# Transposes ahead of the conditioning matmuls, filler matmuls, and two tiny early loads in an adaLN attention and SwiGLU kernel

## The chip, the cores and the metric

The kernel runs on one core of a Trainium2 chip. The metric is device time in microseconds (us) of one execution. The *span* is the time from the first to the last instruction; it is about 2.0 us shorter than the device time. Each timed execution also lists its span and its mean granted TensorE clock (1.000 is full speed).

## The reference, cut to what matters

```
mod = (silu(c) @ w_mod) -> six vectors sa, ca, ga, sb, cb, gb of 1024
h   = layernorm(x) * (1 + ca) + sa                # x: 2048 x 1024
x   = x + ga * linear_attention(h, wqkv, wo)
h   = layernorm(x) * (1 + cb) + sb
x   = x + gb * (silu(h @ w_gate) * (h @ w_up) @ w_down)
```

The study is about the first 27 us: the first four 128-row tiles of x are normalised and transposed, the vectors ca and sa are computed from w_mod as they arrive, and the first matmuls of q begin.

## The kernel before: the parts that matter

All loads go out on the SyncE queue, in this order. None of those shown waits on a computation.

```python
P.dma("c", CS8[0:NDT, :], cv8)
for st in range(4):
    P.dma("x0_%d" % st, XRES[:, st, :], xv[:, st, :])      # 256 KB each, 2 KB rows
...
for p in range(4):
    ca_load(p)        # "wca": 256 columns of the scale part of w_mod, 512 KB in 512-byte rows
    sa_load(p)        # "wsa": the same of the shift part
    if p < 3:
        wq_load(p)    # 512 KB of the q weights, 2 KB rows
```

I number these loads from 0: wca0, wsa0, wq0, ..., wca3, wsa3. The first computations, in TensorE's order:

```python
warm(11, bank=3)                 # filler matmuls, to have the clock granted
mod_sc(WCA, 8, range(2))         # 16 matmuls of one column; wait for wca0
warm(3, bank=3)
... layer norm of tiles 0 and 1 (VectorE), of 2 and 3 (also ScalarE) ...
tile_transposes(0)
...
mod_sc(WSA, 0, range(2))         # wait for wsa0
tile_transposes(1)
...
h0_first(0, 0, "dve")            # scale and shift: the first input of q
...                              # then q matmuls; mod_pair(1), (2), (3) between them
```

`mod_pair(p)` computes the vectors from wca *p* and wsa *p*. TensorE reaches `mod_pair(3)` after the first four of seven column groups of its third pass over q.

## Time and profile before

| | before |
|---|---|
| time, median of 3 | 840.45 us (840.42 to 840.97) |
| span of the profiled execution | 838.5 us |
| TensorE busy | 825.3 us (98%) |
| TensorE's waits for wca in the head | 2.7 us |
| TensorE's waits for wsa in the head | 0.2 us |
| granted clock 9 to 15 us | 0.50 |

This is TensorE's timeline of the kernel before. The columns are start, duration, engine, line, operation, output and inputs, form and count; in brackets stand the idle time before it and what ended it.

```profile
2.76 3.87 PE L178 MATMUL ps<-e_92,ident 128*128 128x512 bf16 x11 [0.37 <-DVE e_92 L178]
9.38 0.59 PE L178 MATMUL ps<-siluc,wca 128*128 128x1 bf16 x16 [2.75 <-DMA wca<-in_w_mod_dram]
...
11.06 1.06 PE L178 MATMUL ps<-ident,xres 128*128 128x128 bf16 x8
11.91 0.61 PE L178 MATMUL ps<-siluc,wsa 128*128 128x1 bf16 x16
12.39 1.01 PE L178 MATMUL ps<-ident,xres 128*128 128x128 bf16 x8
13.59 2.29 PE L178 MATMUL ps<-ht,wqk 128*128 128x256 bf16 x10 [0.19 <-DVE ht L178]
...
26.52 0.55 PE L178 MATMUL ps<-siluc,wsa 128*128 128x1 bf16 x16 [0.18 <-DMA wsa<-in_w_mod_dram]
```

Two things strike the eye: the gap of 2.75 us at 9.38, and the short wait for wsa3 at 26.52.

The next view is a table of stretches of the kernel before: stretch, length, busy time of TensorE, weight loads, VectorE, ScalarE and GpSimd (instructions started), granted clock, DMA share, GB/s.

```profile
4.00:5.00 1.00, 1.00 (x4) 0.43 (x3) 0.95 (x2) 0.00 (x0) 0.00 (x0) 1.00 1.08 227
5.00:6.00 1.00, 1.00 (x5) 0.37 (x4) 1.00 (x3) 0.00 (x0) 0.00 (x0) 1.00 0.85 265
9.00:10.00 1.00, 0.62 (x17) 0.56 (x18) 0.12 (x2) 0.97 (x3) 0.55 (x1) 0.50 1.12 307
14.00:15.00 1.00, 1.00 (x6) 0.72 (x5) 1.00 (x3) 0.46 (x1) 0.00 (x0) 0.50 1.14 318
```

The clock is at half from 9 us on, and the DMA engines are full. (The table counts time before the first clock record as 1.00. The fillers there start 0.43 us apart until 5.5 us and 0.21 us apart afterwards, so the clock was first granted at about 5.5 us.) At 4 to 6 us the stream is slower than later.

The chain of waits, in order of time, says what 26.52 depended on (start, duration, what):

```profile
17.38 0.47 SPq L178
17.85 0.04 issue
17.89 8.58 DMA wsa<-in_w_mod_dram
26.48 0.04 issue
26.52 2.84 PE ps L178 x26
```

Back of 26.52 there is only SyncE's queue and the load.

### The profile page before, as it was taken

The page shows a single profiled execution, that of the slowest core. Times are in us where ns is not written, and L with a number is a line of the kernel's source. Part 1 is how long each engine was busy: PE and PEld are TensorE (multiplying, and loading weights), DVE is VectorE, ACT ScalarE, POOL GpSimd, SP SyncE. Part 2 cuts the span into 40 slices and gives each one's busy share as a digit, 9 for nine tenths or more (in the row PEclk, how much of TensorE's full clock was granted, in tenths as well). Part 3 has the DMA queues.
Part 4 walks back from the last instruction along what each step waited for, and adds up shares of the span by engine and source line. Part 5 has one row for each costly group of instructions (what it writes and reads, how often), then busy time and mean ns, then how long its engine had stood idle before and what let it go on. Part 6 is the DMA issues. An engine that isn't in the chain of part 4 may idle for free.

```text
span 838.5 us, 10210 instructions
## 1 busy us (share of the span) xinstructions
PE 825.3 (98%) x4154; PEld 384.1 (46%) x4233; DVE 298.3 (36%) x641; ACT 203.8 (24%) x355; POOL 41.0 (5%) x52
## 2 busy tenths in 40 slices
PE   7999999999999999999999999999999999999998
PEld 4444444454444444444444444444444444444444
DVE  5777966556974212111221111022121102111111
ACT  4667763213333111100111111021111101111111
POOL 1000000000050000030000003000000300000000
PEclk8999999999999999999999999999999999999999
DMA  9993323747195895540355562045556104553000
GB/s 276 265 323 48 68 89 126 172 136 265 37 248 184 266 296 155 153 80 26 108 153 153 151 157 58 24 114 151 151 150 181 46 13 113 151 152 99 1 25 26
DMA packets 178125, 112.99 MB, mean 135 GB/s; under 512 B 32664, under 2 KB 161824, under 8 KB 178080
## 3 DMA queue, kind: packets, MB, share of 16 engines
q1 hardware_dynamic: 178080, 112.35, 48.1%
q8 instruction: 33, 0.54, 0.3%
q14 instruction: 12, 0.10, 0.0%
HBM read 100.67 MB, written 4.33 MB: 125 GB/s over the span
## 4 chain that ended last, share of the span: by engine, by line
PE 95%; SPq 2%; DMA 1%; DVE 1%; issue 1%; ACT 0%; DVEq 0%
PE ps L178 95%; SPq L178 2%; DMA wsa<-in_w_mod_dram 1%; DVE acc L178 0%; DVE xres L178 0%; DVE mhl L178 0%; ACT mw L178 0%; DVE ve_72 L178 0%; DVE ut L178 0%; DVE mean_70 L178 0%; DVE msq_71 L178 0%; DVE sumx L178 0%; DVEq L249 0%
## 5 line engine op out<-in xcount | busy, mean ns | idle before, releaser
L178 DVE TENSOR_TENSOR at<-sg,ps 128x512 bf16<-128x512 bf16 x112 | 77.0, 688 | 296.1 <-PE ps L178 285.1
L178 ACT ACTIVATE sg<-ps 128x512 bf16<-128x512 f32 x112 | 66.9, 597 | 310.3 <-PE ps L178 298.9
L178 PE MATMUL ps<-wd_a,at 128*128 128x512 bf16 (+2 forms) x519 | 112.8, 372 | 0.5
L178 PE MATMUL ps<-wd_b,at 128*128 128x512 bf16 (+2 forms) x388 | 85.4, 372 | 0.5
L178 PEld LDWEIGHTS ps<-wd_a,at 128*128 128x128 bf16 x528 | 51.1, 98 | 59.8
L178 DVE TENSOR_TENSOR ut<-att,gb_b 128x512 bf16<-128x512 bf16 (+1 forms) x32 | 13.5, 421 | 167.7 <-ACT att L178 167.7
L178 ACT ACTIVATE att<-ps 128x512 bf16<-128x512 f32 (+1 forms) x32 | 17.4, 591 | 182.1 <-PE ps L178 182.1
L178 PE MATMUL ps<-ht,wqk 128*128 128x512 bf16 (+1 forms) x258 | 58.4, 376 | 1.0 <-DVE ht L178 0.5
L178 PEld LDWEIGHTS ps<-wd_b,at 128*128 128x128 bf16 x396 | 38.3, 98 | 44.7
L178 PE MATMUL ps<-wqk,ht 128*128 128x512 bf16 x250 | 56.6, 379 | 0.4
L178 PE MATMUL ps<-mw,pqt 128*128 128x512 bf16 x250 | 55.8, 379 | 0.4
L178 PE MATMUL ps<-h2t,guu_117 128*128 128x512 bf16 x221 | 52.8, 379 | 0.2
L178 PE MATMUL ps<-h2t,guu_115 128*128 128x512 bf16 x219 | 52.6, 379 | 0.3
L178 PE MATMUL ps<-h2t,gug_114 128*128 128x512 bf16 x220 | 52.6, 379 | 0.2
L178 PE MATMUL ps<-h2t,guu_116 128*128 128x512 bf16 x221 | 52.6, 379 | 0.2
L178 PE MATMUL ps<-h2t,gug_111 128*128 128x512 bf16 x220 | 52.5, 379 | 0.2
L178 PE MATMUL ps<-h2t,gug_112 128*128 128x512 bf16 x219 | 52.5, 379 | 0.2
L178 PE MATMUL ps<-h2t,gug_113 128*128 128x512 bf16 x219 | 52.3, 379 | 0.3
L178 PE MATMUL ps<-h2t,guu_118 128*128 128x512 bf16 x217 | 52.1, 379 | 0.3
L178 POOL TENSOR_SCALAR h2t<-h2t,modcol 128x512 bf16<-128x512 bf16 x32 | 28.3, 898 | 394.4 <-DMA h2t<-xn_119 394.4
L178 ACT ACTIVATE e_92<-ps 128x512 bf16<-128x512 f32 x64 | 39.1, 611 | 30.8 <-PE ps L178 27.0
L178 ACT ACTIVATE rl<-ps 128x512 bf16<-128x512 f32 x64 | 38.9, 608 | 0.0
(120 smaller groups left out, 685.5 us busy)
## 6 DMA issues: line engine op xcount, KB each, us to landing
gug_111<-in_B_w_gate_dram SPq DMA_DIRECT2D x14, 512.0 KB, 4.0
guu_115<-in_B_w_up_dram SPq DMA_DIRECT2D x14, 512.0 KB, 5.3
gug_112<-in_B_w_gate_dram SPq DMA_DIRECT2D x14, 512.0 KB, 4.0
guu_116<-in_B_w_up_dram SPq DMA_DIRECT2D x14, 512.0 KB, 5.3
gug_113<-in_B_w_gate_dram SPq DMA_DIRECT2D x14, 512.0 KB, 4.0
guu_117<-in_B_w_up_dram SPq DMA_DIRECT2D x14, 512.0 KB, 5.3
gug_114<-in_B_w_gate_dram SPq DMA_DIRECT2D x14, 512.0 KB, 4.1
guu_118<-in_B_w_up_dram SPq DMA_DIRECT2D x14, 512.0 KB, 5.3
```

Source lines behind the costliest of these rows:

```text
L178: return getattr(e, method)(**kw)
```

## The change

The intent is to use TensorE's idle time ahead of wca0 for both tiles' transposes, to keep its clock with fillers, and to pay the first access to w_mod and wqkv early with two tiny loads ("touches") of 32 bytes of every eighth row. The diff, cut to its core:

```diff
+        P.dma("tm", TOUCH[0:16, 0:8, :], wmv[0:128:8, :, 0:16], queue="act")
+        P.dma("tq", TOUCH[0:16, 8:16, :], wqkvv[0:128:8, :, 0:16], queue="act")
         P.dma("c", CS8[0:NDT, :], cv8)
 ...
-        warm(11, bank=3)
-        mod_sc(WCA, 8, range(2))
-        warm(3, bank=3)
         fa = fin_ca(0)
+        warm(13, bank=3)
 ...
         tile_transposes(0)
+        warm(2, bank=3)
         s1_[2]()
         ln1_rstd1(1)
         s3_[0]()
+        ln1_xn(1)
+        tile_transposes(1)
+        warm(0, bank=3)
+        mod_sc(WCA, 8, range(2))
+        warm(4, bank=3)
 ...
         mod_sc(WSA, 0, range(2))
-        tile_transposes(1)
+        warm(3, bank=3)
 ...   (tile 2 is normalised earlier, one copy moves up; bookkeeping for loads on the ScalarE queue)
```

More of the change, by code (lines that the diff above doesn't have):

```diff
@@ L96 @@
 class _Op:
-    __slots__ = ("idx", "eng", "fn", "deps", "signaled", "count", "semkey", "waits", "ninc", "tag")
+    __slots__ = ("idx", "eng", "fn", "deps", "signaled", "count", "semkey", "waits", "ninc", "tag", "isdma")
     def __init__(self, idx, eng, fn, semkey, ninc, tag):
@@ L109, in __init__ @@
         self.tag = tag
+        self.isdma = semkey.startswith("lane:")
 def _is_ap(v):
@@ L129, in add @@
     def add(self, eng, fn, reads=(), writes=(), lane=None, ninc=1, tag=None):
-        if eng in self.COMPUTE:
-            semkey = eng
-        else:
-            assert lane is not None
-            semkey = "lane:" + lane
+        semkey = eng if lane is None else "lane:" + lane
+        assert eng in self.COMPUTE or lane is not None
         op = _Op(len(self.ops), eng, fn, semkey, ninc, tag)
@@ L165, in add @@
         self.by_eng.setdefault(eng, []).append(op)
-        if eng not in self.COMPUTE:
+        if op.isdma:
             self.dma_ops.append(op)
@@ L211, in resolve @@
         for op in self.ops:
-            if op.eng not in self.COMPUTE and op.fn is not None:
+            if op.isdma and op.fn is not None:
                 op.signaled = True
@@ L216, in resolve @@
             if op.signaled:
-                c = counters.get(op.semkey, 0) + (op.ninc if op.eng in self.COMPUTE else 16 * op.ninc)
+                c = counters.get(op.semkey, 0) + (16 * op.ninc if op.isdma else op.ninc)
                 counters[op.semkey] = c
@@ L236, in resolve @@
                 sn = dict(kn)
-                if op.eng in self.COMPUTE:
+                if not op.isdma:
                     sn[op.semkey] = op.count
@@ L253, in body @@
                     if op.signaled:
-                        if eng in self.COMPUTE:
+                        if not op.isdma:
                             r.then_inc(sems[op.semkey], op.ninc)
@@ L327, in bass_adaLN_cond__linear_attn_block__swiglu_ffn__prompt_kernel @@
         RSTD2 = T("rstd2", SM + 2240, [128, NST], FP32)
+        TOUCH = T("touch", 202 * KB, [128, 16, 16], BF16)
         ZCOL = T("zcol", SM + 2304, [128, NHG], FP32)
@@ L620, in bass_adaLN_cond__linear_attn_block__swiglu_ffn__prompt_kernel @@
         neg_rstd(2)
+        m3[1]()
+        m3[2]()
         fa[0]()
-        ln1_xn(1)
+        ln1_xn(2)
         fa[2]()
-        m3[1]()
+        m3[3]()
         fa[4]()
-        m3[2]()
+        m3[4]()
         mod_sc(WSA, 0, range(2))
-        tile_transposes(1)
-        m3[3]()
-        m3[4]()
+        warm(3, bank=3)
+        neg_rstd(3)
         fa[1]()
-        neg_rstd(3)
+        raw_copy(4, 4, 0, "act")
         fa[3]()
@@ L635, in bass_adaLN_cond__linear_attn_block__swiglu_ffn__prompt_kernel @@
         h0_first(1, 0, "dve")
-        raw_copy(4, 4, 0, "act")
         raw_copy(2, 2, 0, "dve")
-        ln1_xn(2)
         ln1_xn(3)
```

## The prediction

> **What bounds it.** TensorE is busy 825.3 of 838.5 us (busy table); the chain of waits is 95% TensorE. The change touches only the first 27 us, so a few microseconds at most are in play.
>
> In that head, the chain of waits, back from the scaling-vector matmuls at 26.52 us, holds no TensorE work: it is SyncE's queue issuing loads up to 17.89, then the last shift-vector load (wsa, 8.58 us in flight, landing 26.48). The DMA stream binds. The table of stretches agrees: DMA share 1.0 to 1.2 from 7 us on, 290 to 360 GB/s. After 26.5 TensorE never again waits long for data.
>
> TensorE loses time earlier: it idles 2.75 us before 9.38 for the first wca, its granted clock is 0.50 from 9 to 15.3 us, and the ten first 256-wide q matmuls take 2.29 us instead of about 1.1. This loss is already repaid before 26.5: the last wait there, 0.18 us, is for DMA.
>
> **What the change does.**
> - It moves both transposes (1.06 and 1.01 us) ahead of the first wca matmuls, and normalised tiles 1 and 2 earlier on VectorE; it adds 8 filler matmuls (0.43 us cold, 0.22 warm). The 2.75 us gap shrinks to well under 1, so by the Trainium skill, "TensorE: Matmul & The Clock Gate", part 1 (clock granted after about 3.4 us of activity, withdrawn after an idle window), the clock should stay at 1.0 where the trace shows 0.50. The first q matmul should move from 13.59 to about 12.6: wsa0 lands at 11.0, wq0 at 12.5.
> - None of this moves a load: SyncE's loads in the head wait on no compute. TensorE, 1 to 2 us earlier, will wait for wsa1 (16.0), wsa2 (21.5), wsa3 (26.5) instead, 2 to 4 us in sum against 0.2. Worth at the end: 0 us.
> - The touches are 256 descriptors of 32 bytes, 16 per DMA engine. From the packet rates (512 bytes: 16 engines x 1.18 / 566 per us = 33 ns; 2 KB: about 96 ns) I estimate 15 to 35 ns each, 0.25 to 0.55 us per engine, partly in idle time before 2.3 us. The Trainium skill, "DMA: Bandwidth & Descriptors", HWDGE ordering, says the ScalarE queue uses the same 16 engines, so this delays the stream: 0 to 0.4 us. ScalarE's table load and silu slip about 0.9 us, off the path.
> - Possible return: at the first accesses to w_mod (4 to 6 us) the stream runs at 227 to 265 GB/s, against about 300 later: 0.3 to 0.45 us lost. If that is a first-access cost, the touches recover it. More likely it is the issuing of many 512-byte descriptors; I give recovery 35%.
>
> **Sum.** The last wsa landing shifts by about -0.1 us (-0.7 to +0.5). Predicted 840.3 us, 8 in 10 between 839.6 and 841.0. Faster by over 2%: 0.01; within: 0.98; slower: 0.01.
>
> **What would show it.** Granted clock 1.0 in 9 to 15 us (else the fillers failed). First q matmul near 12.6. TensorE waits for wsa of 2 us or more in sum. Last wsa landing within 0.6 us of 26.48, the time moving by the same amount. At 4 to 6 us, about 300 GB/s if touching pays, else 230 to 265.
>
> **What would make it wrong.** The new waits could withdraw the clock near 26 us (+1 to 2 us). The touches could be much slower than estimated and hold up the x loads (+1 us). Or the first-access cost is spread over the whole head, and touching brings 1 us or more.

## The result, and the profile after

The changed kernel took 840.04 us (median of 4, 839.95 to 840.74), against 840.43 (840.24 to 840.97) for the kernel before in the same rounds. The ratio is 0.9996, 95% interval 0.9979 to 1.0013: the same. A ratio is the mean time of one kernel's runs over that of the other's of the same rounds, so not quite the ratio of the medians quoted.

TensorE's timeline of the changed kernel:

```profile
2.75 4.67 PE L176 MATMUL ps<-e_93,ident 128*128 128x512 bf16 x13 [0.36 <-DVE e_93 L176]
7.71 0.62 PE L176 MATMUL ps<-ident,xres 128*128 128x128 bf16 x8 [0.28 <-DVE xres L176]
...
9.24 0.62 PE L176 MATMUL ps<-ident,xres 128*128 128x128 bf16 x8 [0.48 <-DVE xres L176]
9.70 0.54 PE L176 MATMUL ps<-siluc,wca 128*128 128x1 bf16 x16
...
11.28 0.55 PE L176 MATMUL ps<-siluc,wsa 128*128 128x1 bf16 x16 [0.16 <-DMA wsa<-in_w_mod_dram]
...
12.83 1.39 PE L176 MATMUL ps<-ht,wqk 128*128 128x256 bf16 x10 [0.32 <-DVE ht L176]
...
25.99 0.55 PE L176 MATMUL ps<-siluc,wsa 128*128 128x1 bf16 x16 [0.85 <-DMA wsa<-in_w_mod_dram]
```

The gap at 9.38 is gone, the first q matmuls start 0.76 us earlier and take 1.39 in place of 2.29 us, and the wait for wsa3 has grown from 0.18 to 0.85 us. The same stretches as before:

```profile
4.00:5.00 1.00, 1.00 (x4) 0.44 (x3) 0.82 (x2) 0.00 (x0) 0.00 (x0) 1.00 1.02 365
5.00:6.00 1.00, 1.00 (x4) 0.32 (x3) 1.00 (x3) 0.34 (x1) 0.00 (x0) 1.00 1.05 310
9.00:10.00 1.00, 0.76 (x20) 0.76 (x21) 0.79 (x7) 0.66 (x3) 0.42 (x1) 1.00 1.01 316
14.00:15.00 1.00, 1.00 (x18) 0.93 (x16) 0.07 (x1) 0.00 (x0) 0.00 (x0) 1.00 1.04 322
```

Once granted, the clock stays at 1.00. The dip at 4 to 6 us is absent, just as if the touches had paid. The chain of waits of the changed kernel:

```profile
17.53 1.21 SPq L176
18.74 0.04 issue
18.78 7.16 DMA wsa<-in_w_mod_dram
25.94 0.05 issue
25.99 34.04 PE ps L176 x213
```

wsa3 landed 0.54 us earlier (25.94 against 26.48), its matmuls began 0.53 us earlier, and the span fell by 0.5 us, from 838.5 to 838.0. From this pair alone one would credit the touches with 0.5 us. The experiments were made to find out whether that is so.

### The profile page after: what moved, and what is told of

Read it like the earlier page. It is cut to its first block, busy times and chain, and to the rows that moved or that the text cites. A ratio compares the mean times of both kernels' runs of the same rounds, so it can differ in the third digit from the quotient of the medians.

```text
span 838.0 us, 10305 instructions
## 1 busy us (share of the span) xinstructions
PE 830.0 (99%) x4241; PEld 383.5 (46%) x4241; DVE 299.5 (36%) x641; ACT 203.9 (24%) x355; POOL 41.2 (5%) x52
## 4 chain that ended last, share of the span: by engine, by line
PE 96%; SPq 2%; DVE 1%; DMA 1%; issue 0%; ACT 0%; DVEq 0%
PE ps L176 96%; SPq L176 2%; DMA wsa<-in_w_mod_dram 1%; DVE acc L176 0%; DVE xres L176 0%; DVE mhl L176 0%; ACT mw L176 0%; DVE ve_72 L176 0%; DVE ut L176 0%; DVE mean_70 L176 0%; DVE msq_71 L176 0%; DVE sumx L176 0%; DVEq L247 0%
## 5 line engine op out<-in xcount | busy, mean ns | idle before, releaser
L176 ACT ACTIVATE att<-ps 128x512 bf16<-128x512 f32 (+1 forms) x32 | 17.4, 591 | 182.1 <-PE ps L176 182.1
```

Of the source, the lines that this page charges most:

```text
L176: return getattr(e, method)(**kw)
```

## The experiments

Theory: the touches move the load stream, the stream's last wsa sets the end, and the reorder by itself is worth nothing. Rivals: the reorder brings the gain; any early traffic helps; or the stream wanders from execution to execution and the pair above is chance.

### Reading a trace of this kernel with one number

In 13 of the 14 traces, the span less the start of the wsa3 matmuls is 811.97 to 812.07 us, for every kernel (for instance 838.5 - 26.52 before, 838.0 - 25.99 after). All that these kernels differ by has happened by that matmul. I call its start the *wsa3 start*. The fourteenth trace is explained below.

### 1 and 2: the new order without touches, twice

```diff
-        P.dma("tm", TOUCH[0:16, 0:8, :], wmv[0:128:8, :, 0:16], queue="act")
-        P.dma("tq", TOUCH[0:16, 8:16, :], wqkvv[0:128:8, :, 0:16], queue="act")
```

> The new order and the fillers, without the two touches. Theory (the touches alone move the load stream, and the end follows the last wsa landing): 840.4 us as before, first wsa3 matmul near 26.5 us, stream at 4 to 6 us at 225 to 265 GB/s; granted clock 1.0 in 9 to 15 us and first q matmul near 12.8 all the same. Rival (the reorder brings the gain, the stream's change is chance): 840.0 us, wsa3 near 26.0.

The first set gave 841.51 us median (840.32 to 841.95). Three of five executions had a granted clock of 0.998 and spans of 839.4 to 839.9; the other two had 1.000 and 838.2. Neither theory had foreseen that. TensorE's timeline of the profiled one:

```profile
20.80 0.55 PE L176 MATMUL ps<-siluc,wca 128*128 128x1 bf16 x16 [0.51 <-DMA wca<-in_w_mod_dram]
22.34 0.55 PE L176 MATMUL ps<-siluc,wsa 128*128 128x1 bf16 x16 [0.99 <-DMA wsa<-in_w_mod_dram]
22.76 4.87 PE L176 MATMUL ps<-ht,wqk 128*128 128x512 bf16 x14
...
27.86 0.54 PE L176 MATMUL ps<-siluc,wsa 128*128 128x1 bf16 x16
```

and its stretches there:

```profile
19.49:22.91 3.42, 1.92 (x37) 1.17 (x36) 0.00 (x0) 0.00 (x0) 0.00 (x0) 1.00 1.02 308
22.91:26.32 3.41, 3.41 (x9) 1.21 (x8) 1.30 (x7) 0.00 (x0) 0.00 (x0) 0.50 1.08 308
```

TensorE, being early, waited 0.51 us for wca2 and 0.99 us for wsa2. It was busy 1.92 of 3.42 us, and for the next 3.41 us its clock was at half. Fourteen q matmuls took 4.87 us where they take 3.26 at full clock, so TensorE reached wsa3 at 27.86 although it had landed at 26.9. This is the risk that the prediction listed, brought about by the new waits.

Was it this kernel or chance? The same kernel was run again.

> The same kernel as the first run of the new order without touches. If the loss of the clock belongs to this kernel: again about three of five executions at 0.998 and 839.4 to 839.9 us span, median 840.3 to 841.5. If it was chance: spans as the changed kernel, 838.0 to 838.5. In the trace, last x load delivered near 6.2 us and the stream behind the touched kernels by 0.3 us or more, if the touches matter; near 5.8 if that was chance too.

This time it took 840.17 us (839.92 to 840.48), all five clocks at 1.000, spans 837.8 to 838.3. So the loss strikes some executions of the same kernel and not others. With the clock kept, the seven executions without touches have a mean span of 838.11 us; the eight executions of the changed kernel with the clock kept (in the result above and in experiment 5) have 838.23. The touches show no gain in timed executions. The trace did not decide between the two forecasts for the x loads: the stream had moved as many bytes as c and x hold at 6.08 us, between 5.8 and 6.2.

### 3: touches alone, in the old order

The edit keeps the two touch lines and restores the old order of TensorE and VectorE.

> The two touches in the old order. Theory: the stream shows 300 GB/s or more at 4 to 6 us and the last wsa lands near 25.9, but TensorE, with a wait of only 0.18 us there before, is not ready before 26.3: the wait for wsa3 vanishes and the time is 840.2 to 840.3, half of the gain or less. Rival (the touches do nothing): 840.4, wsa3 landing at 26.5, 225 to 265 GB/s at 4 to 6 us. Rival 2 (both parts add independently): 840.0.

It took 840.14 us (839.69 to 841.40), kernel before 840.43; ratio 1.0 (0.9987 to 1.0012). wca0 landed at 8.4 us in place of 9.3, so the early gap was shorter and the clock was just kept. But wsa3 landed at 26.3, only 0.2 us earlier than in the first trace. My expectation that TensorE would not be ready and that the wait would vanish was wrong: with the clock kept it was ready, and waited 0.69 us. One us gained at wca0 had shrunk to 0.2 at wsa3. Four of these five executions had a mean clock of 1.000, against 5 of 32 of the kernel before without touches (counted below): an earlier wca0 may save the clock even in the old order. One set of five is thin evidence, and one of the four has a span of 839.4 all the same.

### 4: touches of tensors that the head does not read

```diff
-        P.dma("tm", TOUCH[0:16, 0:8, :], wmv[0:128:8, :, 0:16], queue="act")
-        P.dma("tq", TOUCH[0:16, 8:16, :], wqkvv[0:128:8, :, 0:16], queue="act")
+        P.dma("tm", TOUCH[0:16, 0:8, :], wgv[0:128:8, :, 0:16], queue="act")
+        P.dma("tq", TOUCH[0:16, 8:16, :], wuv[0:128:8, :, 0:16], queue="act")
```

> The changed kernel, with the same two tiny loads of the same shape on the same queue, but of the gate and up weights, which the head does not read. First-access theory: no return, dip to 225 to 265 GB/s at 4 to 6 us, wsa3 near 26.5, 840.4. Rival (any early traffic on the engines or on a second queue helps): as the changed kernel, 840.0, wsa3 near 26.0.

It took 840.35 us (839.95 to 840.75). Its trace is among the fastest, as the timeline at wsa3 shows:

```profile
25.83 0.55 PE L176 MATMUL ps<-siluc,wsa 128*128 128x1 bf16 x16 [0.94 <-DMA wsa<-in_w_mod_dram]
```

The stream ran at 359 and 309 GB/s at 4 to 6 us, though w_mod had not been touched. The first-access theory expected 225 to 265 GB/s and 26.5, so this trace speaks against it. The median of 840.35 does not: it lies nearer to that theory's 840.4 than to the rival's 840.0. One trace is not enough here, as the next experiment shows; the packets below decide.

### 5: the changed kernel again

No edit.

> The changed kernel once more, as the yardstick of this set. Every theory: 840.0 us, wsa3 near 26.0, 310 to 365 GB/s at 4 to 6 us. If wsa3 is near 26.5 here, the landing time wanders from run to run and no single trace of this set proves anything.

It took 840.49 us (840.13 to 841.78), kernel before 840.43. Four clocks were 1.000; one was 0.998, with a span of 839.8. The profiled execution's timeline at wsa3:

```profile
26.49 0.55 PE L176 MATMUL ps<-siluc,wsa 128*128 128x1 bf16 x16 [0.89 <-DMA wsa<-in_w_mod_dram]
```

That is the wsa3 start of the kernel before, from the changed kernel, with a dip to 203 GB/s at 4 to 5 us. This means that the landing wanders by 0.5 us between executions, and the 0.5 us between the first two traces proves nothing about the touches.

### What the packets say about the dip

The trace records every DMA packet. Adding up the bytes of the SyncE queue in order of completion gives the time by which the engines had moved as many bytes as the loads up to a given one hold ("last x done" and so on). It is a count of bytes: single packets of x end later, up to 7.4 us. The landing itself is later too: a load's semaphore is raised 16 times, for wsa3 in the trace of before from 24.21 to 26.48 us, and the last one counts. These numbers are worked out from those records:

```
trace                    second queue     last x done   wca0 done   wca0 - x   wsa3 done
before                   none             6.27          7.88        1.61       24.58
before again             none             5.82          7.44        1.62       24.05
new order, 1st           none             6.25          7.92        1.67       24.82
new order, 2nd           none             6.08          7.80        1.72       24.37
new order, gaps filled   none             6.32          7.95        1.63       24.68
changed                  touches          5.82          7.45        1.63       24.18
changed again            touches          6.20          7.73        1.53       24.48
touches, old order       touches          5.69          7.31        1.62       24.13
touches elsewhere        other tensors    5.77          7.42        1.65       24.03
```

The first 512 KB of w_mod took 1.53 to 1.72 us after the last x in every trace, touched or not. So w_mod had no first-access cost for a touch to recover, beyond 0.1 us. The packets of 512 bytes, which are those of w_mod, say it more directly: the first starts at 5.65 us in the trace of before, and the first 256 take 27 to 30 ns in the mean in all nine traces, touched or not. So the dip at 4 to 6 us belongs to the x loads. In the trace of before a packet of 2 KB takes 84 ns in the median, but seven that began between 4.0 and 5.1 us took 828 to 1444 ns.

From the last x to wsa3 the stream then took 18.2 to 18.6 us in all nine. The wsa3 landing wanders over 1.1 us in these nine traces, 25.8 to 26.9. Of its parts, the end of x wanders over 0.6 us, the way from there to wsa3 over 0.3, and the time until the last engine's share lands (1.8 to 2.2 us) over 0.4. Slow packets are not the general cause of a late x: in the new order's first trace and with the gaps filled x is as late (6.25, 6.32), and no packet before 7 us took over 0.7 us. What makes it late there is open.

Traces with touches of any tensor have x done somewhat earlier (mean 5.87 against 6.15 us), but the ranges overlap, and experiment 10, also with touches, has 6.08. Whether early traffic on a second queue speeds the x loads is open; the timed spans do not show it.

### 6: the new waits filled

To test the cause of the lost clock, filler matmuls of 0.11 us were put into the new waits of the kernel of experiment 1.

```diff
         def mv_pair(p):
+            gap_fill(3 if p == 2 else 0)
             mod_sc(WCA, 8, range(2 * p, 2 * p + 2))
+            gap_fill({2: 3, 3: 6}.get(p, 0))
             mod_sc(WSA, 0, range(2 * p, 2 * p + 2))
```

> The new order without touches, plus filler matmuls of 0.11 us in the new waits: three ahead of the third wca and three ahead of the third wsa vectors, six ahead of the fourth wsa. Theory (in the run without touches three of five executions lost the clock, because the order's new waits of 0.5 and 1.0 us emptied one activity window; the granted clock of those was 0.998 against 1.000, their spans 839.4 to 839.9): with the waits filled no execution loses the clock, all five show 1.000, spans 838.0 to 838.6, median about 840.3 us. Rival (the clock was lost by chance or for another reason): again some executions at 0.998 with spans above 839.3. Rival 2 (fillers sit on the path): every span some 0.3 to 0.7 us longer than 838.2.

All five clocks were 1.000, as the theory has it, but experiment 2 kept its clock too, without fillers, so this is weak evidence. The time was 840.74 us (840.62 to 841.06), spans 838.5 to 839.0. That is the size that the second rival named, but the trace does not show its reason. This is the timeline of the weight loads at wsa3:

```profile
26.73 0.47 PEld L176 LDWEIGHTS ps<-siluc,wsa 128*128 128x128 bf16 x16 [0.32 <-DMA wsa<-in_w_mod_dram]
```

They waited 0.32 us after those of the last filler, for a wsa3 that landed only at 26.69. In this execution the late landing set the end, and the fillers were not on the path. Why every span of this set is longer stays open.

### 7: the kernel before again

> The kernel before once more, with a trace, for the spread of the load stream without touches. Every theory: span minus the start of the fourth wsa vectors' matmuls 812.0 us. Touches matter: stream slow again at 5 to 6.5 us (205 to 265 GB/s), wsa3 at 26.3 or later. Chance: it may be at 300 GB/s there.

It took 840.66 us (840.39 to 840.71), spans 838.4 to 838.7, in its own set 840.44 for the yardstick. The stream was at about 300 GB/s at 5 to 6.5 us without any touch, which is the answer "chance". Its trace corrects the prediction in another point. wsa3 landed at 26.0 us, but the stretches show another loss of the clock:

```profile
18.26:21.67 3.41, 2.19 (x39) 1.45 (x38) 0.00 (x0) 0.00 (x0) 0.00 (x0) 1.00 1.13 329
21.67:25.09 3.42, 3.20 (x8) 1.18 (x8) 1.30 (x7) 0.00 (x0) 0.00 (x0) 0.50 1.18 317
```

and the timeline shows TensorE's arrival at wsa3:

```profile
26.63 0.54 PE L178 MATMUL ps<-siluc,wsa 128*128 128x1 bf16 x16
```

The clock had been withdrawn at 21.67, and TensorE reached wsa3 at 26.63 with no wait. In this execution of the kernel before, TensorE and not the wsa3 landing set the end, 0.6 us late: its chain goes back over the matmuls at half clock to the landing of wsa2 at 21.06.

### The clock, over all executions

The granted clock changes on a grid of 3.41 us whose position differs from execution to execution. With the grid laid over the 13 traces in which I could place it, the withdrawals in the head all followed a window in which TensorE was busy little:

```
TensorE busy in one window   clock in the next
before           0.34        0.50
experiment 10    0.42        0.50
experiment 1     0.56        0.50
experiment 7     0.64        0.50
experiment 3     0.65        1.00
all others       0.69 up     1.00
```

(The window after the loss in the first trace of before was busy 0.86 and the clock stayed at half for one more.) Busy ends are modelled, so 0.64 and 0.65 do not fix the limit that closely. The closest kept case is this window of experiment 3, in the table of stretches:

```profile
6.87:10.28 3.41, 2.22 (x33) 1.25 (x32) 3.08 (x17) 2.49 (x6) 1.47 (x3) 1.00 1.14 329
```

Counting timed executions by their mean clock: the kernel before was below 1.000 in 27 of 32, the new order (experiments 1, 2, 4, 5 and the changed kernel) in 4 of 24. So the new order, fillers included, does what it was meant for; no run has the one without the other. (The 32 are the yardstick runs of three sets and experiment 7; those of the first round are left out, since their clocks are not all listed. The mean clock does not say where in the span the clock was lost.) But those 27 spans reach only from 838.0 to 839.0. In the first trace the loss came early and was made up by the time of wsa3; in experiment 7 it came later and cost 0.6 us. The 4 have 839.4 to 839.9; in the one that was traced (experiment 1) the clock went at 22.9:

| | executions | median us | mean us | median span | clock lost, spans |
|---|---|---|---|---|---|
| before | 32 | 840.52 | 840.52 | 838.40 | 27, 838.0 to 839.0 |
| new order, all | 24 | 840.34 | 840.50 | 838.20 | 4, 839.4 to 839.9 |

The new order wins about 0.2 us in the median and loses it in the mean. Even the 0.2 us are not clear of the wander: when the 56 spans are dealt out at random to two groups of this size, 8% of the deals differ as much. Nor is every long span a lost clock. Two executions of the kernel before (839.4 and 839.7) and one of experiment 3 (839.4) have a mean clock of 1.000; none of them was traced.

### 8 and 9: the first load 0.45 us earlier

The stream begins with the issue of the first x at 1.25 us, behind the tiny load of c. If the stream sets the end, it should start earlier.

```diff
-        P.dma("c", CS8[0:NDT, :], cv8)
+        P.dma("c", CS8[0:NDT, :], cv8, queue="act")     # ahead of the two touches
```

> The changed kernel with the tiny load of c moved from the SyncE queue to the head of the ScalarE queue, so that the first x load is issued at 0.79 us and not at 1.25. Theory (the stream from the first issue to the last wsa sets the end): all landings 0.4 to 0.45 us earlier, wsa3 near 25.7, span 837.5 to 837.9, median 839.6 us. Rival (the engines' slow first packets set the pace whenever the issue comes): no change, 840.0 to 840.2 us.

> The kernel with the load of c at the head of the ScalarE queue, once more. If its lead of 0.5 us over the kernel before is real: all spans 837.6 to 838.1, median 839.7 to 840.0, ratio to before about 0.9992. If it was the luck of one set: spans spread to 838.5 and the median is 840.2.

The two sets gave 839.93 (839.71 to 840.08) and 839.77 us (839.62 to 839.95), kernel before 840.44 and 840.57; ratios 0.9991 (0.9979 to 1.0004) and 0.9993 (0.9979 to 1.0007). All ten clocks were 1.000 and all ten spans 837.6 to 838.1. Without the touches:

> The same without the two touches. Theory (the touches are worth at most 0.1 to 0.3 us, through the x loads' first packets): within 0.2 us of the kernel with them, 839.8 to 840.1. Rival (the touches carry the gain): 840.2 or more, x loads delivered later by 0.3 us or more.

It took 839.85 us (839.63 to 841.17); four spans of 837.6 to 838.3 with the clock kept, and one of 839.1 without. The touches again carry nothing that I can see. Nor did x come later without them: its bytes were done at 5.50 us, against 5.62 and 5.51 with them. Moving c is the steadiest version found, by about 0.7 us against the pooled median of the kernel before (0.45 us in the median span), though the intervals include 1. The landings did not move as expected: wca0 landed at 8.3 and 8.4 us in the traced executions with touches, but wsa3 at 26.0 and 25.9, not 25.7. In the first trace, x0 was done 0.7 us earlier than in the changed kernel, the last x 0.2.

### 10: wsa3 later on purpose

The changed kernel with two later x loads (512 KB) issued ahead of wca3 and wsa3; nothing is added.

```diff
         for p in range(4):
+            if p == 3:
+                x1_load(0)
+                x1_load(1)
             ca_load(p)
```

> The changed kernel with two of the second x loads (2 x 256 KB) issued ahead of the fourth wca and wsa, nothing added or removed. Theory (the last wsa landing sets the end): 0.5 MB at about 350 GB/s is 1.5 us, wsa3 near 27.5, span near 839.5, median 841.5, and span minus start of its matmuls still 812.0. Rival (TensorE or the other loads pace the head): span within 0.3 us of 838.1.

It took 842.55 us (841.15 to 843.21) where 841.5 was expected, ratio 1.0022 (1.0009 to 1.0034). wsa3 landed at 27.6, as expected. The two executions that kept their clock have spans of 839.3 and 839.4, as expected (839.5). Three lost it (840.7 to 841.2), which I had not expected; the profiled one is of these. Its timeline at wsa3:

```profile
27.65 0.55 PE L176 MATMUL ps<-siluc,wsa 128*128 128x1 bf16 x16 [1.15 <-DMA wsa<-in_w_mod_dram]
```

and the two windows around it, in the table of stretches:

```profile
25.12:28.53 3.41, 1.43 (x35) 1.11 (x36) 0.22 (x3) 0.61 (x2) 0.00 (x0) 1.00 1.08 342
28.53:31.95 3.42, 3.42 (x10) 1.19 (x9) 3.28 (x14) 0.00 (x0) 0.59 (x2) 0.50 1.07 360
```

The waits of 0.87 us for wca3 and 1.15 us for wsa3 emptied a window, and the half clock then fell after wsa3. This is the fourteenth trace, with 841.2 - 27.65 = 813.55 in place of 812.0. That a later wsa3 landing moves the end of the new order by as much, unless the clock is lost, is thereby shown. In 11 of the 14 traces the wsa3 matmuls start within 0.05 us of the landing. In the other three (experiments 1, 7 and 11) TensorE comes later than the load.

### 11: longer rows for the scale part of w_mod

Experiment 8 with wca in two loads of 512 columns (1 KB rows), and ten fillers in place of four ahead of wsa0.

> The same with touches, the scale half of w_mod loaded in two pieces of 512 columns (1 KB rows) in place of four of 256 (512-byte rows), and six more fillers for the longer first wait. Theory (the stream to the last wsa binds, and longer rows run faster: 2 MB at about 330 in place of 290 GB/s is 0.8 us): first q matmul near 14.2 us and yet wsa3 near 25.3, span 837.3 to 837.6, median 839.4. If TensorE's remaining work binds once it starts 1.5 us later: wsa vectors without a wait, span 838.0 to 838.8. Rival (row length makes no difference here): wsa3 at 26.0.

The median was 839.69 us (839.50 to 840.86), the lowest; three spans were 837.4 to 837.6, two 838.6 and 838.8. The traced execution is one of the slow ones. wsa3 landed at 25.6 there, but the timeline has:

```profile
26.57 0.54 PE L176 MATMUL ps<-siluc,wsa 128*128 128x1 bf16 x16
```

TensorE came without a wait, 1 us after the landing. Its wsa0 matmuls had begun at 12.64 though wsa0 landed at 11.8, because the ten fillers ran without a gap from 10.48 until then. But that delay was used up before the end: TensorE waited 0.54 us for wsa2, which landed at 22.61, later than in the changed kernel (21.04), and worked without a pause from there to 26.57. Both theories are partly right: the stream got shorter (17.4 us from the last x to wsa3, against 18.2 to 18.6), and in the traced execution wsa2 and TensorE's work after it became the limit.

## Why the prediction was right

- **The time** (840.3, range 839.6 to 841.0) held: 840.04 measured, and the pooled median of the changed kernel's nine executions is 840.21. The range also holds the kernel before (840.43), so the hit by itself tests little. The reason, that the last wsa landing decides and the reorder cannot move that load, is confirmed by experiment 10 and by both traces of the changed kernel, with waits of 0.85 and 0.89 us for wsa3. The constant 812.0 shows only that the end follows the start of these matmuls, whatever released them.
- **"Worth at the end: 0 us"** was read off one execution. In that one, DMA came last at 26.52; in experiment 7, TensorE did, and there an order that keeps the clock could have gained up to 0.6 us (an estimate from that trace: 26.63 against a landing at 26.0). Over 32 and 24 executions the new order's median span is 0.2 us shorter, which is not clear of the wander, and its mean time is the same. So 0 stands.
- **The clock** stayed at 1.00 in the changed kernel's first trace, as predicted from the Trainium skill, "TensorE: Matmul & The Clock Gate", part 1. The listed risk, that new waits withdraw it near 26 us at a cost of 1 to 2 us, came true in 4 of 24 executions of the new order, with spans 1.2 to 1.8 us above the 838.15 of the others' median.
- **First q matmul** near 12.6: 12.83 measured. **Waits for wsa**, 2 to 4 us predicted: 1.3 us. TensorE's other waits took part of the rest: 0.8 us for normalised tiles, which the prediction had left out.
- **The touches' cost** was overestimated: 15 to 35 ns per packet predicted, about 9 ns measured (288 records in all, 2.5 us over 16 engines, 0.16 us each).
- **"At the first accesses to w_mod (4 to 6 us)"** was a misreading. In that stretch the x loads were still running. The packet records put the first packet of w_mod at 5.65 us and show no slower start of w_mod in untouched kernels. The faster stretch in the trace after looked like the recovery to which I had given 35%, and experiments 4 and 5 show that it was not.
- **The net shift** of -0.1 us (-0.7 to +0.5) covered what happened (-0.5 in the first pair, 0 in the repeat), but the wander of the stream is the greater part of it. That the shift fell inside the range is therefore partly luck.

What stays open: why x is late in some executions, and why single x packets take over 1 us in two of the traces (before and changed); whether any early traffic shortens that; and why gains at wca0 shrink on the way to wsa3. In each of the 14 traces a 16 KB packet of the queue labelled "instruction" took 1.1 to 1.2 us, starting at 16.8 to 19.5 us. The engine that carries this packet may then come last, whichever was last before. In experiment 3 fifteen of the 16 signals of wsa3 had come by 25.02 us and the last came at 26.29, later by about the length of that packet, and the first trace of the new order shows the same (25.62 and 26.89). The trace of before and the changed kernel's first have no such single straggler. This is an argument, not a test.

## What to carry to other kernels

Before moving work off an engine's idle time, find which wait ends last in that stage: an engine made faster there only waits longer, and the longer wait can itself cost its clock. When the effect sought is as small as the wander between executions, repeat the unchanged and the changed kernel with a trace before believing a mechanism that fits the first pair. A dip in a rate belongs to whatever bytes were moving then; count the bytes before naming the tensor.

## What the Trainium skill lacked or had wrong

- "TensorE: Matmul & The Clock Gate", part 1, says that the clock is withdrawn after an idle window. Here a window need not be idle: four windows of 3.41 us in which TensorE was busy for 0.34 to 0.64 of the time cost the clock, windows at 0.65 and above did not. (The page also tells of a kernel in which short idle times between groups of matmuls cost the clock, but gives no busy share.) That the grid runs freely and has 3.41 us agrees.
- The same page gives a practical limit of about 3.4 us for a gap. Two waits of 0.51 and 0.99 us in one window sufficed (experiment 1).
- "DMA: Bandwidth & Descriptors" says in "Issuing engines are not separate DMA queues" that issuing from several engines saves only issue time. The runs agree for the stream as a whole: moving one load of 2 KB off the SyncE queue started the first x 0.46 us earlier and the median span is 837.95 us over ten executions, against 838.1 over the changed kernel's nine.
- No page tells of single slow packets in a stream of loads: in the trace of before, seven 2 KB packets of the x loads took 828 to 1444 ns, against 84 ns in the median.
